# Output projection summed in one PSUM bank, a shorter last weight part, and first loads issued ahead of the block

## The chip, the cores and the metric

The kernel runs on one core of one Trainium2 chip. The metric is the device time of one execution in microseconds (us), as the median of several runs. The profile's span is about 1.8 us shorter than the device time (198.66 against 200.44 us for the profiled run of the kernel before).

## The reference

One decoding step of attention with a sliding window: 32 sequences, 32 query heads, 8 key/value heads, of which the last 512 of 2048 positions are used.

```python
B, Sq, D = 32, 1, 512;  Hq, Hkv, Sk, Dh = 32, 8, 2048, 128;  W = 512
q = (x @ wq).reshape(B, Sq, Hq, Dh).transpose(0, 2, 1, 3)
k = repeat(k_cache[:, :, Sk - W:, :], 4, axis=1); v = ...   # the same for v
p = softmax(einsum("bhqd,bhkd->bhqk", q, k) * Dh ** -0.5)
o = einsum("bhqk,bhkd->bhqd", p, v)
return o.transpose(0, 2, 1, 3).reshape(B, Sq, Hq * Dh) @ wo       # 32 x 4096 @ 4096 x 512
```

Every input byte is used once: 64 MB (of 2**20 bytes) of cache window and 4 MB each of wq and wo, 75.5 million bytes in all.

## The kernel before

All loads go through one queue, that of the sync engine (SP): x, four parts of wq, then K and V of each sequence in 512 KB pieces, last four parts of wo with 8 heads each.

```python
block = es.enter_context(nc.Block())
...
@block.sync
def _(sp):
    sp.dma_start(x_sb[:, :], x.rearrange("b s d -> b (s d)")).then_inc(sem_x, 16)
    for kt in range(DKT):
        sp.dma_start(wq_sb[:, kt, :], wq[kt * P:(kt + 1) * P, :]).then_inc(sem_wq[kt], 16)
    ...                                   # K and V, one sequence after the other
    for c in range(4):
        sp.dma_start(wo_sb[:, c * 8:(c + 1) * 8, :],
                     wo[c * 1024:(c + 1) * 1024, :].rearrange("(h d) n -> d h n", d=P)).then_inc(sem_wo[c], 16)
    sp.wait_ge(act_out, 1)
    sp.dma_start(out.rearrange("b s d -> b (s d)"), out_sb[:, :]).then_inc(sem_out, 16)
```

The output projection gives each of the four 32-column groups of the PE array a quarter of the heads. So four partial sums of 32x512 stand in four PSUM banks. They are evicted to X_sb by two engines, and a matmul with R_sb (four 32x32 identities one above the other, made by POOL at the start) adds them up; one more eviction makes the output tile.

```python
for hq in range(HQ):
    c = hq % 4
    if hq % 8 == 0:
        pe.wait_ge(sem_wo[hq // 8], 16)
    ins = pe.matmul(KT_ps[:, c, :].bitcast(F32)[32 * c:32 * (c + 1), :],
                    lhsT=oT_sb[:, :, hq], rhs=wo_sb[:, hq, :],
                    start=(hq < 4), stop=(hq >= HQ - 4), tile_position=(0, 32 * c))
ins.then_inc(pe_fin, 1)
...                                       # wait for the evictions
pe.matmul(QO_ps[0:32, :], lhsT=R_sb[:, :], rhs=X_sb[:, :], start=True, stop=True, ...).then_inc(pe_out, 1)
# DVE evicts groups 0 and 1 to X_sb, ACT groups 2 and 3; ACT then copies QO_ps to out_sb
```

## Time and profile before

| | before |
|---|---|
| device time, median of 3 runs | 200.41 us (200.28 to 200.49) |
| span of the profile | 198.7 us |
| read from HBM | 75.53 MB, about 408 GB/s in mid-kernel |
| last wo part releases PE | 192.86 us |
| from there to the issue of the output DMA | 3.86 us |
| from that issue to the end of the span | 1.94 us |

The first parts of the profile's page, kernel before. In the slice rows each digit (or number) stands for 1/40 of the span; digits are tenths, PEclk is the clock granted to PE in tenths.

```profile
span 198.7 us, 5891 instructions
## 1 busy us (share of the span) xinstructions
PE 142.8 (72%) x2597; PEld 111.8 (56%) x2597; DVE 100.8 (51%) x188; ACT 58.3 (29%) x70; POOL 13.3 (7%) x46
## 2 busy tenths in 40 slices
...
PEclk9999999699999969988998799969996797855555
DMA  5999999999999999999999999999999999999930
GB/s 181 424 418 411 409 407 412 403 411 407 408 411 403 409 407 407 410 407 409 406 407 410 407 413 403 408 407 407 411 406 411 401 409 406 410 396 334 344 133 7
```

DMA is at 9 in every slice from the second to the 38th, and the traffic is flat at about 408 GB/s up to the 35th. In the wo load after that it falls to 396, 334 and 344 GB/s, although DMA is as busy: wo comes in 4096 packets of 1 KB, 0.050 us each on average in the trace, K and V in packets of 4 KB, 0.163 us each. No compute engine is busy as steadily as that: the kernel is bound by its input stream. The chain of work that ended last, by engine and by line, says the same: it is issue of DMAs on the sync queue and DMAs.

```profile
...
SPq 50%; DMA 28%; PE 14%; DVE 3%; issue 2%; ACT 1%; DVEq 0%
SPq L132 24%; DMA K_sb<-in_k_cache_dram 23%; SPq L140 18%; PE KT_ps L236 9%; SPq L151 7%; DMA w_sb<-in_wo_dram 6%; PE S_ps L253 2%; DVE P_ex L359 2%; PE QO_ps L286 1%; SPq L126 1%; DVE KT_sb L337 1%; PE PT_ps L268 1%; PE KT_ps L308 1%; ACT P_f L407 0%; DVEq L45 0%
```

The change looks for time in two places: in the head, before the stream is full, and in the tail, after the last wo byte. The timeline of the head (start us, length us, engine, line, operation, tiles; in brackets the idle time before and what ended it):

```profile
...
0.74 0.39 SPq L124 DMA_DIRECT2D x_sb<-in_x_dram  x1
...
1.19 2.23 SPq L126 DMA_DIRECT2D w_sb<-in_wq_dram  x4
...
2.84 0.29 DVE L325 CAST xT_sb<-S_ps 128x128 bf16<-128x128 f32 x1 [2.84 <-PE S_ps L203]
...
6.18 1.02 PE L214 MATMUL PT_ps<-xT_sb,w_sb 128*128 128x32 bf16 x32 [3.37 <-DMA w_sb<-in_wq_dram]
```

The x load holds the sync queue first, so the first wq part is issued at 1.19 us. It releases PE at 6.18 us. The CAST line: a 128x128 copy out of PSUM takes 0.29 us on DVE. The tail:

```profile
...
190.17 1.08 PE L308 MATMUL KT_ps<-w_sb,oT_sb 128*32 128x512 bf16 x8 [1.85 <-DMA w_sb<-in_wo_dram]
...
192.86 1.08 PE L308 MATMUL KT_ps<-w_sb,oT_sb 128*32 128x512 bf16 x8 [1.61 <-DMA w_sb<-in_wo_dram]
193.99 1.20 ACT L431 ACTIVATE X_sb<-KT_ps 32x512 bf16<-32x512 f32 x2 [15.38 <-PE KT_ps L308]
194.00 1.39 DVE L382 CAST X_sb<-KT_ps 32x512 bf16<-32x512 f32 x2 [10.15 <-PE KT_ps L308]
...
195.49 0.59 PE L318 MATMUL QO_ps<-X_sb,R_sb 128*32 128x512 bf16 x1 [1.54 <-DVE X_sb L382]
196.11 0.59 ACT L435 ACTIVATE out_sb<-QO_ps 32x512 bf16<-32x512 f32 x1 [0.91 <-PE QO_ps L318]
196.72 0.36 SPq L156 DMA_DIRECT2D out_dram<-out_sb  x1
```

After the last release at 192.86 come two rounds of four 512-column matmuls, the four evictions (two per engine), the summing matmul, one more eviction, and the output issue. The data of wo's last part arrive on 16 DMA engines ("lanes" below). In the trace's semaphore updates, the fastest lane had its share at 189.60 and the slowest at 192.82; PE can only start after the slowest.

The DMA issues of the page (size of each, median us from issue to landing):

```profile
...
w_sb<-in_wo_dram SPq DMA_DIRECT2D x4, 1024.0 KB, 17.6
x_sb<-in_x_dram SPq DMA_DIRECT2D x1, 32.0 KB, 1.7
out_dram<-out_sb SPq DMA_DIRECT2D x1, 32.0 KB, 1.5
```

### The profile page before, as it was taken

How to read it: one execution, taken by the hardware profiler on the slowest of the kernel's cores; microseconds unless marked ns; L12 is line 12 of the kernel's file. 1: busy time of each engine (PE TensorE's matmuls, PEld its weight loads, DVE VectorE, ACT ScalarE, POOL GpSimd, SP SyncE). 2: the span in 40 equal slices, each digit the busy share in tenths (PEclk: the TensorE clock that was granted, in tenths of full speed). 3: DMA queues.
4: the chain of work that ended last, by engine and by line, in shares of the span. 5: the costliest groups of instructions: out<-in, count | busy, mean ns of one | idle time of the engine just before them, and what ended most of it. 6: DMA issues, size and time to landing. Idle time of an engine off the chain costs nothing.

```text
span 198.7 us, 5891 instructions
## 1 busy us (share of the span) xinstructions
PE 142.8 (72%) x2597; PEld 111.8 (56%) x2597; DVE 100.8 (51%) x188; ACT 58.3 (29%) x70; POOL 13.3 (7%) x46
## 2 busy tenths in 40 slices
PE   0448996797787799759776977697769697647431
PEld 0337874776565568556755666566656485537000
DVE  0004579755853577335943595359435944531002
ACT  2001345333252325204522343233423251130003
POOL 8202000000000001000000000000000000000000
PEclk9999999699999969988998799969996797855555
DMA  5999999999999999999999999999999999999930
GB/s 181 424 418 411 409 407 412 403 411 407 408 411 403 409 407 407 410 407 409 406 407 410 407 413 403 408 407 407 411 406 411 401 409 406 410 396 334 344 133 7
DMA packets 23289, 75.95 MB, mean 382 GB/s; under 512 B 2208, under 2 KB 6368, under 8 KB 22752
## 3 DMA queue, kind: packets, MB, share of 16 engines
q1 hardware_dynamic: 23264, 75.57, 96.6%
q8 instruction: 21, 0.34, 0.7%
q14 instruction: 4, 0.03, 0.0%
HBM read 75.53 MB, written 0.03 MB: 380 GB/s over the span
## 4 chain that ended last, share of the span: by engine, by line
SPq 50%; DMA 28%; PE 14%; DVE 3%; issue 2%; ACT 1%; DVEq 0%
SPq L132 24%; DMA K_sb<-in_k_cache_dram 23%; SPq L140 18%; PE KT_ps L236 9%; SPq L151 7%; DMA w_sb<-in_wo_dram 6%; PE S_ps L253 2%; DVE P_ex L359 2%; PE QO_ps L286 1%; SPq L126 1%; DVE KT_sb L337 1%; PE PT_ps L268 1%; PE KT_ps L308 1%; ACT P_f L407 0%; DVEq L45 0%
## 5 line engine op out<-in xcount | busy, mean ns | idle before, releaser
L236 PE MATMUL KT_ps<-perm,K_sb 128*128 128x128 bf16 x1024 | 75.8, 238 | 22.6 <-DMA K_sb<-in_k_cache_dram 22.4
L337 DVE COPY KT_sb<-KT_ps 128x1024 bf16<-128x1024 bf16 x96 | 63.7, 687 | 53.2 <-PE KT_ps L236 52.9
L236 PEld LDWEIGHTS KT_ps<-perm,K_sb 128*128 128x128 bf16 x1024 | 67.0, 107 | 29.2 <-DMA K_sb<-in_k_cache_dram 26.7
L399 ACT ACTIVATE KT_sb<-KT_ps 128x1024 bf16<-128x1024 bf16 x32 | 32.8, 1024 | 83.0 <-PE KT_ps L236 83.0
L286 PEld LDWEIGHTS QO_ps<-PT_sb,V_sb 128*128 128x128 bf16 x1024 | 28.2, 98 | 17.4 <-issue 13.9
L286 PE MATMUL QO_ps<-PT_sb,V_sb 128*128 128x16 bf16 x1024 | 31.2, 171 | 2.4 <-ACT PT_sb L417 1.2
L359 DVE TENSOR_SCALAR P_ex<-P_f,recip 32x512 bf16<-32x512 f32 x32 | 25.3, 791 | 1.1
L253 PE MATMUL S_ps<-KT_sb,QBD 128*32 128x512 bf16 x256 | 22.7, 437 | 0.0
L417 ACT ACTIVATE PT_sb<-PT_ps 128x1024 bf16<-128x1024 bf16 x16 | 15.5, 1021 | 19.1 <-PE PT_ps L268 19.1
L268 PE MATMUL PT_ps<-ident,P_ex 128*128 128x128 bf16 x128 | 9.7, 236 | 10.6 <-DVE P_ex L359 10.6
L196 POOL COPY QBD<-QT_sb 128x32 bf16<-128x32 bf16 x32 | 7.9, 261 | 117.6 <-PE S_ps L253 108.6
L268 PEld LDWEIGHTS PT_ps<-ident,P_ex 128*128 128x128 bf16 x128 | 8.2, 106 | 11.5 <-DVE P_ex L359 11.5
L366 DVE CAST oT_sb<-QO_ps 128x32 bf16<-128x32 f32 x32 | 5.9, 183 | 9.5 <-PE QO_ps L286 9.4
L214 PE MATMUL PT_ps<-xT_sb,w_sb 128*128 128x32 bf16 x128 | 4.1, 188 | 7.6 <-DMA w_sb<-in_wq_dram 7.6
L308 PE MATMUL KT_ps<-w_sb,oT_sb 128*32 128x512 bf16 x32 | 4.3, 637 | 6.0 <-DMA w_sb<-in_wo_dram 6.0
L214 PEld LDWEIGHTS PT_ps<-xT_sb,w_sb 128*128 128x128 bf16 x128 | 3.7, 104 | 8.0 <-DMA w_sb<-in_wq_dram 4.6
L343 DVE TENSOR_REDUCE maxv<-S_ps 128x1 f32<-128x512 f32 x8 | 5.5, 691 | 5.2 <-PE S_ps L253 5.2
L407 ACT ACTIVATE P_f<-S_ps,negmax 128x512 f32<-128x512 f32 x8 | 5.5, 688 | 6.8 <-DVE negmax L345 6.8
L382 DVE CAST X_sb<-KT_ps 32x512 bf16<-32x512 f32 x2 | 1.4, 680 | 10.2 <-PE KT_ps L308 10.2
L329 DVE CAST QT_sb<-PT_ps 128x512 bf16<-128x512 f32 x1 | 0.7, 692 | 11.5 <-PE PT_ps L214 11.5
L253 PEld LDWEIGHTS S_ps<-KT_sb,QBD 128*32 128x32 bf16 x256 | 4.0, 97 | 4.0 <-issue 1.6
L308 PEld LDWEIGHTS KT_ps<-w_sb,oT_sb 128*32 128x32 bf16 x32 | 0.9, 149 | 8.7 <-DMA w_sb<-in_wo_dram 7.9
(27 smaller groups left out, 15.2 us busy)
## 6 DMA issues: line engine op xcount, KB each, us to landing
K_sb<-in_k_cache_dram SPq DMA_DIRECT2D x64, 512.0 KB, 15.6
V_sb<-in_v_cache_dram SPq DMA_DIRECT2D x64, 512.0 KB, 15.4
w_sb<-in_wq_dram SPq DMA_DIRECT2D x4, 1024.0 KB, 7.9
w_sb<-in_wo_dram SPq DMA_DIRECT2D x4, 1024.0 KB, 17.6
x_sb<-in_x_dram SPq DMA_DIRECT2D x1, 32.0 KB, 1.7
out_dram<-out_sb SPq DMA_DIRECT2D x1, 32.0 KB, 1.5
```

The lines of the kernel that those rows point to most:

```text
L132: sp.dma_start(K_sb[:, b % NK, h].rearrange("p r d -> p (r d)"), cache_rows(k_cache, b, h)).then_inc(sem_k[b % NK][h], 16)
L140: sp.dma_start(V_sb[:, b % NV, h].rearrange("p r d -> p (r d)"), cache_rows(v_cache, b, h)).then_inc(sem_v[b % NV], 16)
L151: sp.dma_start(wo_sb[:, c * 8:(c + 1) * 8, :], wo[c * 1024:(c + 1) * 1024, :].rearrange("(h d) n -> d h n", d=P),).then_inc(sem_wo[c], 16)
L196: pool.tensor_copy(dst, src).then_inc(pool_qbd, 1)
L236: ins = pe.matmul(KT_ps[:, t, i * 128:(i + 1) * 128], lhsT=K_sb[:, b % NK, h, 8 * (t % 2) + i, :], rhs=perm[:, :, :], start=True, stop=Tru ...
L253: ins = pe.matmul(S_ps[32 * c:32 * c + 32, :], lhsT=QBD[:, b % NQB, g, :], rhs=KT_sb[:, b % NKT, h, :, c, :], start=(j == 0 and h == 0), s ...
L268: ins = pe.matmul(PT_ps[:, r // 8, (r % 8) * 128:(r % 8 + 1) * 128], lhsT=P_ex[:, r, :, :].rearrange("p s g -> p (s g)"), rhs=ident[:, :], ...
L286: ins = pe.matmul(QO_ps[:, 16 * h:16 * h + 16], lhsT=V_sb[:, b % NV, h, r, :], rhs=PT_sb[:, q % 2, r, :].rearrange("p (c n) -> p c n", c=G ...
L337: dve.tensor_copy(KT_sb[:, b % NKT, t // 2, 8 * (t % 2):8 * (t % 2) + 8, :, :], KT_ps[:, t, :]).then_inc(dve_T, 1)
L359: dve.tensor_scalar(P_ex[rows, :, :, c], P_f32[rows, :].rearrange("p (r s) -> p r s", r=NR), recip[rows, q:q + 1], None, op0=ALU.mult,).th ...
L399: act.activation(KT_sb[:, b % NKT, 1, 8:16, :, :], KT_ps[:, 3, :], ACTF.Copy).then_inc(act_T, 1)
L417: act.activation(PT_sb[:, q % 2, 8 * i:8 * i + 8, :].rearrange("p r n -> p (r n)"), PT_ps[:, i, :], ACTF.Copy,).then_inc(act_PT, 1)
```

## The change

Its intent is to shorten both ends. The four column groups now divide the 512 output columns and not the heads: every head is multiplied into four blocks of 128 columns, all summed in one PSUM bank. No partial sums are left to be added, and one 128x128 copy evicts the result. The last wo part is cut to 4 heads. The x load moves to the ACT queue, and wq's first part goes first on the sync queue, both ahead of the block. The output leaves as 128 rows of 256 bytes.

```diff
+    WO_CUT = (0, 10, 20, 28, 32)
-        X_sb = ...   R_sb = ...            # and POOL's work for R_sb, the semaphores of the sum
-        out_sb = sb("out_sb", [32, D], BF16)
+        out_sb = sb("out_sb", [P, 128], BF16)
+        nc.scalar.dma_start(x_sb[:, :], x.rearrange("b s d -> b (s d)")).then_inc(sem_x, 16)
+        nc.sync.dma_start(wq_sb[:, 0, :], wq[0:P, :]).then_inc(sem_wq[0], 16)
         block = es.enter_context(nc.Block())
...
-            sp.dma_start(x_sb[:, :], x.rearrange("b s d -> b (s d)")).then_inc(sem_x, 16)
-            for kt in range(DKT):
+            for kt in range(1, DKT):
...
+                h0, h1 = WO_CUT[c], WO_CUT[c + 1]
                 sp.dma_start(
-                    wo_sb[:, c * 8:(c + 1) * 8, :],
+                    wo_sb[:, h0:h1, :],
...
-            sp.dma_start(out.rearrange("b s d -> b (s d)"), out_sb[:, :]).then_inc(sem_out, 16)
+            sp.dma_start(
+                out.rearrange("b s (c n) -> c (b s) n", c=4), out_sb[:, :]
+            ).then_inc(sem_out, 16)
...
             for hq in range(HQ):
-                c = hq % 4
-                ins = pe.matmul(KT_ps[:, c, :]...[32 * c:32 * (c + 1), :], ..., rhs=wo_sb[:, hq, :], ...)
+                for c in range(4):
+                    ins = pe.matmul(
+                        KT_ps[:, 0, :].bitcast(F32)[32 * c:32 * (c + 1), 0:128],
+                        lhsT=oT_sb[:, :, hq],
+                        rhs=wo_sb[:, hq, c * 128:(c + 1) * 128],
+                        start=(hq == 0), stop=(hq == HQ - 1), tile_position=(0, 32 * c),
+                    )
             ins.then_inc(pe_fin, 1)
-            pe.matmul(QO_ps[0:32, :], lhsT=R_sb[:, :], rhs=X_sb[:, :], ...).then_inc(pe_out, 1)
...
-            # two evictions on DVE, two on ACT, then QO_ps to out_sb on ACT
+            dve.tensor_copy(out_sb[:, :], KT_ps[:, 0, :].bitcast(F32)[:, 0:128]).then_inc(dve_out, 1)
```

More of the change, by code (lines that the diff above doesn't have):

```diff
@@ L64, in bass_standalone__sliding_block_cached__sampling_kernel @@
         perm = sb("perm", [P, G4, NS], BF16)
-        X_sb = sb("X_sb", [P, D], BF16)
-        R_sb = sb("R_sb", [P, 32], BF16)
         x_sb = sb("x_sb", [32, D], BF16)
-        out_sb = sb("out_sb", [32, D], BF16)
+        out_sb = sb("out_sb", [P, 128], BF16)
         maxv = sb("maxv", [P, NQUAD], F32)
@@ L91, in bass_standalone__sliding_block_cached__sampling_kernel @@
         pe_PV = sem("pe_PV")
-        pe_out = sem("pe_out")
         pe_fin = sem("pe_fin")
-        dve_x = sem("dve_x")
-        act_x = sem("act_x")
-        pool_R = sem("pool_R")
         pool_perm = sem("pool_perm")
@@ L109, in bass_standalone__sliding_block_cached__sampling_kernel @@
         act_PT = sem("act_PT")
-        act_out = sem("act_out")
+        dve_out = sem("dve_out")
         act_warm = sem("act_warm")
@@ L150, in _ @@
             for c in range(4):
+                h0, h1 = WO_CUT[c], WO_CUT[c + 1]
                 sp.dma_start(
-                    wo_sb[:, c * 8:(c + 1) * 8, :],
-                    wo[c * 1024:(c + 1) * 1024, :].rearrange("(h d) n -> d h n", d=P),
+                    wo_sb[:, h0:h1, :],
+                    wo[h0 * DH:h1 * DH, :].rearrange("(h d) n -> d h n", d=P),
                 ).then_inc(sem_wo[c], 16)
-            sp.wait_ge(act_out, 1)
-            sp.dma_start(out.rearrange("b s d -> b (s d)"), out_sb[:, :]).then_inc(sem_out, 16)
+            sp.wait_ge(dve_out, 1)
+            sp.dma_start(
+                out.rearrange("b s (c n) -> c (b s) n", c=4), out_sb[:, :]
+            ).then_inc(sem_out, 16)
             sp.wait_ge(sem_out, 16)
@@ L175, in _ @@
             pool.memset(P_ex[:, :, :, :], 0.0).then_inc(pool_ex, 1)
-            pool.wait_ge(pool_init, 2)
-            pool.tensor_tensor(R_sb[:, :], ident[:, 0:32], ident[:, 32:64], ALU.add).then_inc(pool_R, 1)
-            pool.wait_ge(pool_R, 1)
-            pool.tensor_tensor(R_sb[:, :], R_sb[:, :], ident[:, 64:96], ALU.add).then_inc(pool_R, 1)
-            pool.wait_ge(pool_R, 2)
-            pool.tensor_tensor(R_sb[:, :], R_sb[:, :], ident[:, 96:128], ALU.add).then_inc(pool_R, 1)
             pool.wait_ge(pool_init, 4)
@@ L304, in _ @@
             for hq in range(HQ):
-                c = hq % 4
-                if hq % 8 == 0:
-                    pe.wait_ge(sem_wo[hq // 8], 16)
-                ins = pe.matmul(
-                    KT_ps[:, c, :].bitcast(F32)[32 * c:32 * (c + 1), :],
-                    lhsT=oT_sb[:, :, hq],
-                    rhs=wo_sb[:, hq, :],
-                    start=(hq < 4), stop=(hq >= HQ - 4), tile_position=(0, 32 * c),
-                )
-            ins.then_inc(pe_fin, 1)
-            pe.wait_ge(pool_R, 3)
-            pe.wait_ge(dve_x, 2)
-            pe.wait_ge(act_x, 2)
-            pe.matmul(
-                QO_ps[0:32, :], lhsT=R_sb[:, :], rhs=X_sb[:, :], start=True, stop=True, tile_position=(0, 0),
-            ).then_inc(pe_out, 1)
+                if hq in WO_CUT:
+                    pe.wait_ge(sem_wo[WO_CUT.index(hq)], 16)
+                for c in range(4):
[5 more added lines that the diff above has]
+                    )
+            ins.then_inc(pe_fin, 1)
         @block.vector
@@ L380, in _ @@
             dve.wait_ge(pe_fin, 1)
-            for c in range(2):
-                dve.tensor_copy(
-                    X_sb[32 * c:32 * (c + 1), :], KT_ps[:, c, :].bitcast(F32)[32 * c:32 * (c + 1), :]
-                ).then_inc(dve_x, 1)
+            dve.tensor_copy(out_sb[:, :], KT_ps[:, 0, :].bitcast(F32)[:, 0:128]).then_inc(dve_out, 1)
         @block.scalar
@@ L428, in _ @@
                     pt_evac((it - 5) // 4)
-            act.wait_ge(pe_fin, 1)
-            for c in range(2, 4):
-                act.activation(
-                    X_sb[32 * c:32 * (c + 1), :], KT_ps[:, c, :].bitcast(F32)[32 * c:32 * (c + 1), :], ACTF.Copy
-                ).then_inc(act_x, 1)
-            act.wait_ge(pe_out, 1)
-            act.activation(out_sb[:, :], QO_ps[0:32, :], ACTF.Copy).then_inc(act_out, 1)
 _INS = ['x', 'k_cache', 'v_cache', 'wq', 'wo']
```

## The prediction

> **What bounds it now.** Input traffic. In the 40-slice rows DMA is at 9 from slice 2 to slice 38 and the core moves about 408 GB/s; PE is busy 72%, DVE 51%. The chain of waits is 50% DMA issue and 28% DMA, ending with the wo load. So only two stretches can be shortened: the head before the stream is full, and the tail after the last wo byte.
>
> Head (timeline): the opening barrier is left at 0.66 us; the sync queue issues x at 0.74 and the first wq part only at 1.19; that part releases the projection at 6.15.
>
> Tail (timeline; clock 0.5 throughout): wo parts release PE at 184.35, 187.24, 190.17 and 192.86. After the last: 8 matmuls of 512 columns until 193.95, four evictions of 0.59-0.68 us on two engines until 195.39, the summing matmul 195.49-196.08, one eviction of 0.59 us, output issue at 196.72, end 198.7. From release to output issue is 3.86 us.
>
> **What changes.**
> 1. Last part 4 heads instead of 8. In the trace one round of four column groups x 512 columns takes 0.44 us (second round starts 193.30 after 192.86), so the groups run concurrently; a round of 128 columns is an estimated 0.11 us. Four rounds plus about 0.2 us of pipeline: 0.65 us instead of 1.09. The third part lands about 1.35 us before the last and needs 8 rounds, about 1 us: no backlog. 96 matmuls more, off the critical path.
> 2. The evictions, the summing matmul and the last eviction (2.7 us with hand-overs) become one 128x128 CAST from PSUM. The same shape at the head (xT) takes 0.29 us; with hand-overs 0.37. Release to output issue: about 1.05 us, a gain of 2.8.
> 3. The output leaves as 128 rows of 256 bytes instead of 32 of 1 KB, and its outermost dimension is 4. The Trainium skill ("DMA: Bandwidth & Descriptors", "Why a DMA increments its semaphore by 16 and not by 1") says that the number of DMA engines is the largest up to 16 that divides both outermost sizes: here 4 engines with 32 rows each. Its "Specifications" ask at least 512 bytes for line rate. No run shows this yet. In this trace a 1 KB output row takes about 0.05 us, a 4-byte packet 0.009; I estimate 0.025 per 256-byte row: +0.5 us, perhaps +0.2 to +1.3. The skill does not help the other way: this cost is the main uncertainty.
> 4. The first wq part goes first on the sync queue, x goes on the ACT queue. The loads still stand behind the opening barrier, so being ahead of the block itself gives nearly nothing; the gain is the x issue slot, 0.45 us. As the stream stays full and total bytes are the same, it carries to the last wo byte.
>
> The slowest DMA lanes still set the last wo landing; cutting it differently does not move it. R_sb and its adds on POOL are off the path.
>
> **Sum.** 0.45 + 2.8 - 0.5 = 2.75 us. 200.41 becomes 197.6 us; range 196.9 to 198.8. Faster by over 2%: 0.05; within 2%: 0.94; slower: 0.01.
>
> **What would show it.** First wq part releases PE near 5.7; last wo release near 192.4; from there to the output issue about 1.05 us; CAST about 0.29; output from issue to landing about 2.0 instead of 1.5; last PE burst 0.65.
>
> **What would make it wrong.** Output rows costing much more than 0.025 us each; x on the other queue slowing the first wq part, so that the head gains nothing; four column groups in one PSUM bank not running concurrently (the scores already do so, at 89 ns per 512-column matmul); a third part still being worked when the last lands.

## The result, and the profile after

The changed kernel took 198.02 us (median of 4 runs, 197.91 to 198.32) against 200.36 us (200.28 to 200.49) for the kernel before on the same chip. The ratio is 0.9885 (95% interval 0.9868 to 0.9902). A ratio is the mean time of one kernel's fast runs over that of the other's in the same rounds, so not quite the ratio of the medians quoted here. The gain is 2.34 us, within 2%, and inside the predicted range; it is 0.4 us short of the predicted 2.75.

The page after, the rows of the stream:

```profile
span 196.5 us, 6073 instructions
...
## 2 busy tenths in 40 slices
...
DMA  5999999999999999999999999999999999999970
GB/s 205 425 417 409 411 405 409 411 409 405 409 409 405 408 407 409 410 407 410 404 409 408 409 409 404 410 406 409 406 408 408 408 409 403 409 404 350 338 253 16
```

The stream is as fast as before, with the same fall in the wo load (350 and 338 GB/s). The chain is issue and DMA even more than it was (89% against 78%); after the last wo landing it holds only PE's last burst (0.68 us) and DVE's CAST (0.29 us):

```profile
...
SPq 52%; DMA 37%; PE 7%; issue 2%; DVE 0%
DMA K_sb<-in_k_cache_dram 32%; SPq L136 25%; SPq L128 18%; SPq L148 8%; DMA w_sb<-in_wo_dram 5%; PE KT_ps L229 4%; PE QO_ps L279 1%; PE S_ps L246 1%; SPq L122 1%; PE KT_ps L301 0%; SPq L110 0%; DVE out_sb L368 0%
```

The head after:

```profile
...
0.73 0.40 ACTq L109 DMA_DIRECT2D x_sb<-in_x_dram  x1
...
0.74 0.41 SPq L110 DMA_DIRECT2D w_sb<-in_wq_dram  x1
...
4.37 0.29 DVE L312 CAST xT_sb<-S_ps 128x128 bf16<-128x128 f32 x1 [4.37 <-PE S_ps L196]
...
6.22 1.01 PE L207 MATMUL PT_ps<-xT_sb,w_sb 128*128 128x32 bf16 x32 [1.89 <-DMA w_sb<-in_wq_dram]
```

wq's first part is issued at 0.74 instead of 1.19 us, but PE was released by it at 6.22, no earlier than before (6.18). The tail after:

```profile
...
191.62 1.08 PE L301 MATMUL KT_ps<-w_sb,oT_sb 128*32 128x128 bf16 x32 [1.41 <-DMA w_sb<-in_wo_dram]
...
192.95 0.65 PE L301 MATMUL KT_ps<-w_sb,oT_sb 128*32 128x128 bf16 x16 [0.25 <-DMA w_sb<-in_wo_dram]
193.66 0.29 DVE L368 CAST out_sb<-KT_ps 128x128 bf16<-128x128 f32 x1 [10.70 <-PE KT_ps L301]
193.97 0.69 SPq L153 DMA_DIRECT2D out_dram<-out_sb  x1
```

The last burst is 0.65 us, the CAST 0.29, and the output is issued 1.02 us after the release instead of 3.86. The third part's burst ends at 192.70, 0.25 us before the last part comes, so there was no backlog. The DMA issues after:

```profile
...
w_sb<-in_wo_dram SPq DMA_DIRECT2D x2, 1280.0 KB, 19.3
w_sb<-in_wo_dram SPq DMA_DIRECT2D x1, 1024.0 KB, 12.7
w_sb<-in_wo_dram SPq DMA_DIRECT2D x1, 512.0 KB, 9.9
x_sb<-in_x_dram ACTq DMA_DIRECT2D x1, 32.0 KB, 3.2
out_dram<-out_sb SPq DMA_DIRECT2D x1, 32.0 KB
```

No landing time stands behind the output's line any more. In the trace its semaphore has five update records, one 0.22 us before the first row starts and four after the last row, where the kernel before had sixteen. The Trainium skill states this case ("DMA: Bandwidth & Descriptors", "Why a DMA increments its semaphore by 16 and not by 1"): a DMA runs on the largest number of engines up to 16 that divides the outermost sizes of both sides, and the issuing engine itself writes the missing increments at once. Here the sizes are 4 and 128, and the trace agrees: four updates came with the data.

The profiled executions give three terms; the second and third are the same within 0.01 us in all three profiles of the changed kernel:

| us | before | after | difference |
|---|---|---|---|
| last wo part releases PE | 192.86 | 192.95 | +0.09 |
| release to output issue | 3.86 | 1.02 | -2.84 |
| output issue to end of span | 1.94 | 2.56 | +0.62 |
| span | 198.66 | 196.53 | -2.13 |

The third term was predicted at +0.5, the second at -2.8. The open question is the first: it was predicted at -0.45.

### The profile page after: what moved, and what is told of

Its sections match the earlier page's. It is cut to its first block, busy times and chain, and to the rows that moved or that the text cites. A ratio compares the mean times of both kernels' runs of the same rounds, so it can differ in the third digit from the quotient of the medians.

```text
span 196.5 us, 6073 instructions
## 1 busy us (share of the span) xinstructions
PE 142.8 (73%) x2692; PEld 116.4 (59%) x2692; DVE 99.8 (51%) x187; ACT 56.5 (29%) x67; POOL 12.1 (6%) x43
## 4 chain that ended last, share of the span: by engine, by line
SPq 52%; DMA 37%; PE 7%; issue 2%; DVE 0%
DMA K_sb<-in_k_cache_dram 32%; SPq L136 25%; SPq L128 18%; SPq L148 8%; DMA w_sb<-in_wo_dram 5%; PE KT_ps L229 4%; PE QO_ps L279 1%; PE S_ps L246 1%; SPq L122 1%; PE KT_ps L301 0%; SPq L110 0%; DVE out_sb L368 0%
## 5 line engine op out<-in xcount | busy, mean ns | idle before, releaser
L246 PE MATMUL S_ps<-KT_sb,QBD 128*32 128x512 bf16 x256 | 21.4, 414 | 0.0
L261 PE MATMUL PT_ps<-ident,P_ex 128*128 128x128 bf16 x128 | 11.8, 266 | 9.6 <-DVE P_ex L346 9.6
L261 PEld LDWEIGHTS PT_ps<-ident,P_ex 128*128 128x128 bf16 x128 | 10.1, 122 | 10.7 <-DVE P_ex L346 10.7
L189 POOL COPY QBD<-QT_sb 128x32 bf16<-128x32 bf16 x32 | 7.4, 245 | 117.9 <-PE S_ps L246 108.0
L301 PE MATMUL KT_ps<-w_sb,oT_sb 128*32 128x128 bf16 x128 | 4.3, 313 | 6.6 <-DMA w_sb<-in_wo_dram 6.6
L301 PEld LDWEIGHTS KT_ps<-w_sb,oT_sb 128*32 128x32 bf16 x128 | 3.3, 158 | 7.4 <-DMA w_sb<-in_wo_dram 4.7
```

What stands on the lines that cost most here:

```text
L246: ins = pe.matmul(S_ps[32 * c:32 * c + 32, :], lhsT=QBD[:, b % NQB, g, :], rhs=KT_sb[:, b % NKT, h, :, c, :], start=(j == 0 and h == 0), s ...
L261: ins = pe.matmul(PT_ps[:, r // 8, (r % 8) * 128:(r % 8 + 1) * 128], lhsT=P_ex[:, r, :, :].rearrange("p s g -> p (s g)"), rhs=ident[:, :], ...
```

## The experiments

Twelve runs stood in three groups; each group stood on one chip and shared its runs of the kernel before. In about half of the kernels the profiled execution, the first of its kernel, was the slowest, by 0.1 to 0.3 us over the next, so the head is judged by the times of all runs and not by one profile.

### Group 1: the head

Theory 1: the head gained next to nothing, because x on a second queue interleaves with the first wq packets and makes some lanes late. Rival: the head gained what was predicted, and something in the tail ate it.

**The changed kernel again** (no edit), as the yardstick.

> The changed kernel again, as the yardstick of this group of runs on one chip. Ratio to before 0.9885 as in its first run (198.0 us); last wo part releasing PE between 192.5 and 193.0.

Measured: 197.98 us (197.82 to 198.12), ratio 0.9877 (0.9863 to 0.9890); kernel before 200.43 us. Release of PE by the last wo part at 192.74.

**Only the head undone.**

```diff
-        nc.scalar.dma_start(x_sb[:, :], ...)
-        nc.sync.dma_start(wq_sb[:, 0, :], ...)
...
-            for kt in range(1, DKT):
+            sp.dma_start(x_sb[:, :], ...)
+            for kt in range(DKT):
```

> The changed kernel with only its head undone: x first on the sync queue and wq part 0 behind it, both inside the block as before. Theory 1 (the head gained next to nothing because x on the second queue interleaves with the first wq packets and two lanes start late): same time as the changed kernel, within 0.15 us. Rival (the head gain of 0.45 us is there and something else in the tail ate it, such as the new cut of wo): 0.35 to 0.5 us slower than the changed kernel.

Measured: 198.34 us (198.31 to 198.53), ratio 0.9897. That is 0.36 us slower than the yardstick, by the means 0.41 (198.38 against 197.97), and no run of one lies among the runs of the other. Theory 1's "next to nothing" falls: the head is worth about 0.4 us, though the first pair of profiles did not show it. Its interleaving comes back under group 3.

**Only the head changed**, on the kernel before (the same lines, the other way round).

> The kernel before with only the head changed (x on the ACT queue, wq part 0 on the sync queue, both ahead of the block). Theory 1: within 0.2 us of before (ratio 0.999 to 1.001). Rival: 0.35 to 0.5 us faster than before (ratio about 0.998).

Measured: 200.14 us (200.12 to 200.42) against 200.43, ratio 0.9985 (0.9971 to 0.9998). The means differ by 0.27 us. The slowest of the five runs was the profiled one; the other four lie below every run of the kernel before. This lies between what the two theories expected, nearer to the rival.

**x behind wq's first part on one queue**, on the changed kernel.

```diff
-        nc.scalar.dma_start(x_sb[:, :], ...)
         nc.sync.dma_start(wq_sb[:, 0, :], ...)
+        nc.sync.dma_start(x_sb[:, :], ...)
```

> The changed kernel with x moved from the ACT queue to the sync queue behind wq part 0, so that no second queue interleaves. Theory 1: all 16 lanes of wq part 0 have landed by about 5.6 us (6.08 in the changed kernel), and the kernel ends 0.3 to 0.45 us earlier than the changed one. Rival (the first packets of the stream are slow until about 3.3 us whatever is issued when): wq part 0 still lands at 6.0 and the time is that of the changed kernel.

Measured: 198.00 us (197.94 to 198.21), ratio 0.9880, the same as the yardstick. The head of its timeline:

```profile
...
0.74 0.40 SPq L109 DMA_DIRECT2D w_sb<-in_wq_dram  x1
...
1.20 0.41 SPq L110 DMA_DIRECT2D x_sb<-in_x_dram  x1
...
6.10 0.26 PE L196 MATMUL S_ps<-ident,x_sb 32*128 32x32 bf16 x4 [6.10 <-DMA x_sb<-in_x_dram]
```

PE gets x only at 6.10 us instead of 2.54 in the kernel before, and the kernel is none the slower: the work that waits for x has slack. But its slowest lane of wq part 0 had landed at 5.75, and the yardstick's at 5.76. On this chip there was nothing for the single queue to mend, and the second queue was not needed for the gain: it is enough that wq's first part goes before x.

### Group 2: the tail

This group ran on another chip, and the changed kernel was not in it; this chip seems to differ: the one kernel that also ran on another, that with 1 KB rows, took 198.33 us here (197.67 to 198.73) and 197.83 there (197.78 to 197.86), with nearly the same time of the kernel before (200.44 and 200.53). So the times of this group decide little.

**wo in four equal parts**, on the changed kernel.

```diff
-    WO_CUT = (0, 10, 20, 28, 32)
+    WO_CUT = (0, 8, 16, 24, 32)
```

> The changed kernel with wo in four equal parts of 8 heads as before. Theory (the last part's size only shortens the last PE burst): last burst 8 rounds, about 1.08 us instead of 0.65, last landing unmoved, 0.43 us slower than the changed kernel (ratio to before about 0.990). Rival (bigger early parts also make the last bytes land later, by 0.2 to 0.3 us): the last part lands earlier here and the net loss is only 0.1 to 0.2 us.

Measured: 198.80 us (198.62 to 199.01), ratio 0.9916. The last burst and what follows:

```profile
...
193.17 1.08 PE L301 MATMUL KT_ps<-w_sb,oT_sb 128*32 128x128 bf16 x32 [1.58 <-DMA w_sb<-in_wo_dram]
194.31 0.29 DVE L368 CAST out_sb<-KT_ps 128x128 bf16<-128x128 f32 x1 [11.33 <-PE KT_ps L301]
194.63 0.69 SPq L153 DMA_DIRECT2D out_dram<-out_sb  x1
```

The burst is 1.08 us instead of 0.65 and release to issue 1.46 us instead of 1.02: the shorter last part is worth 0.44 us, as its theory says. The rival, that an equal cut lets the last bytes land earlier, found no support: they landed at 193.13, in step with this execution's late start (see the table of lanes below). The rest of the time difference cannot be attributed, for want of a yardstick on this chip.

**Output rows one after the other** (relative error 1.37). Its output is wrong, which doesn't matter for the time.

```diff
-                out.rearrange("b s (c n) -> c (b s) n", c=4), out_sb[:, :]
+                out.rearrange("b s (c n) -> (b s c) n", c=4), out_sb[:, :]
```

> Wrong result on purpose: the changed kernel, but the 128 output rows of 256 bytes go to the output one after the other instead of column block by column block, so the outermost size of both sides is 128. Same bytes, same row size, same count. Theory (the output is slow because only 4 DMA engines take it, 32 rows each): 16 engines with 8 rows each, issue near 0.4 us, first to last packet about 0.2 us, issue to end about 2.0 us instead of 2.55, kernel about 0.5 us faster than the changed one. Rival (256-byte writes to HBM are slow in themselves): packets of 0.018 us become no rarer in cost, issue to end stays within 0.15 us of 2.55.

Measured: 197.99 us (197.78 to 198.01), ratio 0.9873. The tail:

```profile
...
193.05 0.65 PE L301 MATMUL KT_ps<-w_sb,oT_sb 128*32 128x128 bf16 x16 [0.22 <-DMA w_sb<-in_wo_dram]
193.76 0.29 DVE L368 CAST out_sb<-KT_ps 128x128 bf16<-128x128 f32 x1 [10.94 <-PE KT_ps L301]
194.08 0.36 SPq L153 DMA_DIRECT2D out_dram<-out_sb  x1
```

Same rows, same bytes, but 16 engines: the issue takes 0.36 us instead of 0.69, and issue to end 1.91 us instead of 2.56. In the trace's packets the first row starts 0.86 us after the issue instead of 1.29, and from first to last row it takes 0.26 instead of 0.52 us. So the 0.62 us of the changed output goes with the four engines, in two shares: the issue of 32 rows on each of four engines takes 0.33 us longer, and the rows then pass more slowly (in the steady part of the trace they start in fours, a four every 0.014 us). The edit also makes the destination contiguous, which is a second difference; but the four-DMA run below keeps the 1 KB stride on 16 engines and has its first row 0.86 us after the issue too, so the stride is not what delayed the first row. For the spacing of the rows the two were not separated. Rows of 256 bytes by themselves cost nothing here: 1.91 us against 1.94 for the 1 KB rows of the kernel before. The total time did not show the expected gain of 0.5 us: the ratio 0.9873 stands against 0.9876 to 0.9885 for the changed kernel on other chips. In this profile the last wo part released PE late, at 193.05, but the profiled run was also the fastest of the four (197.78 us), so this is no full answer, and without a yardstick on this chip it stays open. Group 3 shows on the clock what 16 engines gain.

**Four copies side by side, output in 1 KB rows.**

```diff
-            dve.tensor_copy(out_sb[:, :], KT_ps[:, 0, :].bitcast(F32)[:, 0:128]).then_inc(dve_out, 1)
+            for c in range(2):            # groups 2 and 3 the same on ACT
+                dve.tensor_copy(out_sb[:, c * 128:(c + 1) * 128],
+                                KT_ps[:, 0, :].bitcast(F32)[32 * c:32 * (c + 1), 0:128]).then_inc(dve_out, 1)
...
-                out.rearrange("b s (c n) -> c (b s) n", c=4), out_sb[:, :]
+                out.rearrange("b s d -> b (s d)"), out_sb[:, :]         # out_sb is 32 x 512 again
```

> The changed kernel with the eviction done as four 32x128 copies that move the column groups side by side into a 32x512 tile, two on DVE and two on ACT, and the output sent as 32 rows of 1 KB as before. If the output costs what theory says: release to issue grows by about 0.3 us (two copies one after the other on each engine), issue to end falls from 2.55 to 1.95, net 0.3 us faster than the changed kernel (ratio to before about 0.9865). Rival: the copies cost as much as the output saves, no difference.

Measured: 198.33 us (197.67 to 198.73, five runs), ratio 0.9886, which missed the expectation. Its durations are as expected: release to issue 1.36 us, issue to end 1.94. What was lost was lost at the start of the profiled run:

```profile
...
0.73 0.42 ACTq L110 DMA_DIRECT2D x_sb<-in_x_dram  x1
...
0.74 0.41 SPq L111 DMA_DIRECT2D w_sb<-in_wq_dram  x1
...
5.22 0.27 PE L196 MATMUL S_ps<-ident,x_sb 32*128 32x32 bf16 x4 [5.22 <-DMA x_sb<-in_x_dram]
...
6.79 1.01 PE L207 MATMUL PT_ps<-xT_sb,w_sb 128*128 128x32 bf16 x32 [1.30 <-DMA w_sb<-in_wq_dram]
```

x reached PE at 5.22 us and wq's first part only at 6.79, 0.57 us later than in the first profile of the changed kernel; its slowest lane landed at 6.66.

**Output as four DMAs**, two on each queue, 32 rows of 256 bytes each.

```diff
-            sp.dma_start(out.rearrange("b s (c n) -> c (b s) n", c=4), out_sb[:, :]).then_inc(sem_out, 16)
+            for c in (0, 1):              # c = 2 and 3 on the ACT queue
+                sp.dma_start(out.rearrange("b s d -> b (s d)")[:, c * 128:(c + 1) * 128],
+                             out_sb[32 * c:32 * (c + 1), :]).then_inc(sem_out, 16)
```

> The changed kernel with the output as four DMAs of 32 rows of 256 bytes, two on the sync queue and two on the ACT queue; each has 32 as its outermost size on both sides. Theory: 16 engines each; the second issue starts about 0.4 us after the first, end about 1.95 us after that: issue to end about 2.35 instead of 2.55, 0.1 to 0.3 us faster than the changed kernel. Rival (small rows are what costs): no gain or a loss.

Measured: 198.20 us (197.87 to 198.39), ratio 0.9885; issue to end 2.51 us, so almost nothing of the gain came. The rows themselves were done 1.54 us after the first issue, but the trace shows the 64 updates of the one semaphore (16 of each DMA) coming one after the other from 195.01 to 195.89 us, one every 0.014 us; the last comes 0.56 us after the rows are done. With one DMA of 16 updates the series takes 0.22 us (198.03 to 198.25 in the kernel before). The expected gain seems to have gone into this wait; a semaphore for each DMA was not tried.

### What ties the end to the start

For every profile, the moment when the slowest lane had landed its share of wq's first part, and that of wo's last part:

| profile | wq part 0, slowest lane | wo last part, slowest lane | between |
|---|---|---|---|
| before | 6.04 | 192.82 | 186.78 |
| changed, first run | 6.08 | 192.91 | 186.83 |
| changed, group 1 | 5.76 | 192.69 | 186.93 |
| head undone | 6.12 | 193.11 | 186.99 |
| head only | 6.03 | 192.79 | 186.76 |
| x behind wq0 | 5.75 | 192.54 | 186.79 |
| equal parts | 6.24 | 193.13 | 186.89 |
| output flat | 6.30 | 193.01 | 186.71 |
| 1 KB rows | 6.66 | 193.58 | 186.92 |
| four output DMAs | 5.94 | 192.72 | 186.78 |

The distance is the same within 0.3 us, while the start varies by 0.9. With the four profiles of group 3 added, the distance to the end varies by 0.29 us when counted from the slowest lane of wq part 0, by 0.66 from the mean of its lanes and by 0.99 from the fastest. So the end moves with the slowest lane's start. This is what the prediction's "carries to the last wo byte" comes to, with one correction: what carries is the slowest lane's start, not the issue time. It fits that the first profile showed no head gain (6.08 against 6.04). Why it carries is not shown. The trace does not name the engine of a packet, so whether the same lane is last at both ends is not known, and the lanes drift apart on the way: x behind wq part 0 on the third chip starts with its lanes within 0.30 us and ends with them 3.45 us apart, the 1 KB rows here start 1.20 us apart and end at 3.64.

### Group 3: a square of two choices on one chip

To see whether x on the second queue causes the late lanes, and whether the 1 KB output pays, both choices were crossed on a third chip.

> The changed kernel, first corner of a square of two choices on one chip: x on the ACT queue or behind wq part 0 on the sync queue; output as 128 rows of 256 bytes or as 32 rows of 1 KB. Ratio to before about 0.988. In all ten profiles so far the slowest lane of wo's last part landed 186.7 to 187.0 us after the slowest lane of wq part 0; that should hold here too.

> Second corner: x behind wq part 0, output as changed. If x on the second queue is what makes a lane late at the start (in the profile of the 1 KB output version its packets took up to 0.8 us and wq part 0 landed at 6.66), this lands wq part 0 by 5.8 and is 0.2 to 0.4 us faster than the first corner, with less scatter. Rival (the lateness is chance, whatever the queue): same time as the first corner, as it was on the other chip.

> Third corner: x on the ACT queue, output as 32 rows of 1 KB. From its profile (release to issue 1.36 instead of 1.02, issue to end 1.94 instead of 2.56) 0.28 us faster than the first corner; its first timing did not show that because its wq part 0 landed late.

> Fourth corner: both. The output saves 0.28 us; with theory on x another 0.2 to 0.4: 197.3 to 197.5 us, ratio 0.985 to 0.986, the fastest of all. Rival: 0.28 us below the first corner only.

Measured (kernel before: 200.53 us, 200.36 to 200.63):

| | output as changed | output in 1 KB rows |
|---|---|---|
| x on the ACT queue | 198.02 (197.96 to 198.18), ratio 0.9876 | 197.83 (197.78 to 197.86), ratio 0.9865 |
| x behind wq part 0 | 198.05 (197.88 to 198.12), ratio 0.9874 | 197.70 (197.63 to 197.75), ratio 0.9859 |

The slowest lanes fit the table above: 186.71 to 186.99 us in ten profiles, 186.75, 186.96, 186.75 and 186.76 us here. The 1 KB rows pay 0.19 and 0.35 us (expected 0.28). x behind wq part 0 pays nothing in the first column, where the rival's "same time" held, and 0.13 us in the second, where 0.2 to 0.4 us were expected. So the fourth corner missed its 197.3 to 197.5 us; and on this chip, as on the first, the second queue cost little or no time. What the three profiles with x on one queue behind wq share is an even start (slowest lane at 5.75, 5.71 and 5.73), while the nine with x on the ACT queue range from 5.76 to 6.66. All 14 profiles side by side do show the interleaving of theory 1: the longest x packet took 0.35 to 1.28 us in the nine with x on the ACT queue, and 0.05 to 0.11 us in the five with x on the sync queue. The lanes of wq part 0 landed within 0.30 to 0.46 us of each other in those five, but 0.65 to 1.20 us apart in seven of the nine. Each profile is a single execution, and in the medians of the two chips the effect hardly shows. Whether the second queue causes the scatter on the second chip stays open: x behind wq part 0 was never run there.

The tail of the fastest kernel, x behind wq part 0 with 1 KB rows:

```profile
...
193.24 0.57 ACT L418 ACTIVATE out_sb<-KT_ps 32x128 bf16<-32x128 f32 x2 [15.00 <-PE KT_ps L301]
193.24 0.59 DVE L369 CAST out_sb<-KT_ps 32x128 bf16<-32x128 f32 x2 [9.77 <-PE KT_ps L301]
193.89 0.36 SPq L155 DMA_DIRECT2D out_dram<-out_sb  x1
```

The two copies on each engine take 0.57 and 0.59 us where the single CAST takes 0.29, and the output's issue falls back to 0.36. It beats the changed kernel's runs on this chip without overlap, by 0.32 us, and the kernel before by 2.8 us; its interval against before, 0.9844 to 0.9873, touches that of the changed kernel (0.9861 to 0.9891).

## Why the prediction was right or wrong

The total was right: 197.6 us predicted with a range of 196.9 to 198.8, 198.02 measured, and a change within 2%.

1. **What bounds it** was right: the stream is at 408 GB/s in both kernels until the wo load, and only the two ends moved. That "only two stretches can be shortened" overlooked the wo load itself, at 334 to 344 GB/s.
2. **Last part of 4 heads**: predicted 0.65 us instead of 1.09, measured 0.65 instead of 1.08; the equal cut gave the 1.08 back. The four groups do run side by side in one bank: in the trace the rounds follow each other every 0.107 us (0.11 estimated).
3. **One CAST in place of evictions, sum and eviction**: predicted 0.29 us and about 1.05 us from release to issue, measured 0.29 and 1.02. Of the 2.84 us won between release and issue (2.8 predicted), 2.41 are this step (from the last matmul's end to the issue 2.77 us before and 0.36 after) and 0.43 the one above. Together they are more than the kernel's whole gain. No run undoes this step alone; but the tail as a whole (head undone against the kernel before, by the means of group 1) is worth 2.08 us on the clock, and its terms in the profiles, 2.84 - 0.62, give 2.22.
4. **The output**: predicted +0.5 us with four engines, measured +0.62. The mechanism was right: the flat output's profile gives it all back, and the 1 KB rows of group 3 win 0.19 and 0.35 us on the clock. That the size came so near was partly luck, because two errors worked against each other. The term counted only the rows, and too much for them (0.025 us each was guessed, 0.014 was measured; from first to last row it took 0.26 us more than on 16 engines). It left out the later start: the issue grew from 0.36 to 0.69 us and the first row came 0.43 us later. (The "about 0.05 us" given for a 1 KB output row is low: the 32 rows took 0.063 us on average in the trace.)
5. **The head**: predicted 0.45 us, with the signs "first wq part releases PE near 5.7; last wo release near 192.4". The first profile showed neither (6.22 and 192.95), and in no profile did wq's first part release PE before 5.89 us; but the times show a gain of 0.41 us when the head is undone and 0.27 us when it alone is done. So the step "the gain is the x issue slot, 0.45 us ... it carries to the last wo byte" was right in direction and a little too large; it overlooked that lanes do not start together, and that the end moves with the slowest one. That being ahead of the block is worth nearly nothing agrees with the traces: the first DMA is issued at 0.74 us in both kernels, and no run undid this part alone.

The sum of the measured terms, -2.84 + 0.62 - 0.27 to 0.41, is -2.5 to -2.6 us; the groups measured -2.3 to -2.5. The difference, up to 0.3 us, is of the size of the scatter of the slowest lane, and is not settled.

## What to carry to other kernels

In a kernel bound by one stream, as this one is, the work after the last byte is the compute to shorten first, and it is best found by listing the chain from the last landing to the end: choose the layout of the last matmul so that nothing is left to add up, and make the last part small. Look at the outermost size of both sides of an output DMA before changing its layout: here 4 instead of 32 cost 0.62 us of the 2.84 won. Read the start and end of such a stream by its slowest lane and by the times of many runs; one profile per kernel hid a gain of 0.3 to 0.4 us.

## What the Trainium skill lacked or had wrong

- "DMA: Bandwidth & Descriptors", "Why a DMA increments its semaphore by 16 and not by 1": right on the number of engines (outermost sizes 4 and 128 gave 4 updates with the data), but it gives no time for the price of few engines: the issue took 0.69 us instead of 0.36, and the first row started 1.29 us after it instead of 0.86.
- "DMA: Bandwidth & Descriptors", "Specifications", asks for at least 512 bytes for line rate: 128 output rows of 256 bytes on 16 engines took 1.91 us from issue to end, against 1.94 for 32 rows of 1 KB. At 32 KB the row size cost nothing; the measurement decides for this size.
- "DMA: Bandwidth & Descriptors", "Anatomy of one DMA — SWDGE (gpsimd) path", calls the semaphore write essentially free. It speaks of DMAs issued from gpsimd, so it is not refuted here; what it lacks for DMAs issued from SP and ACT is that the updates of one semaphore came one every 0.014 us, 0.22 us for one DMA's 16 and 0.88 us for the 64 of four DMAs that share it.
- "DMA: Bandwidth & Descriptors", "Issuing engines are not separate DMA queues", says that a second issuing engine saves only the issue time. The runs agree: the head saved 0.27 to 0.41 us of an issue slot of 0.45, and x behind wq part 0 on one queue was as fast (198.00 against 197.98 us). It gives no cost of their interleaving: the longest x packet on the second queue took 0.35 to 1.28 us, on the sync queue 0.05 to 0.11.
- No page that was read tells that the end of a long stream moves with the slowest lane of its first load: the slowest lane of wo's last part landed 186.7 to 187.0 us after the slowest lane of wq part 0 in all 14 profiles, while the fastest lane of wo's last part was done up to 3.8 us earlier (189.21 against 193.01).
